# Block-causal attention and a three-way maximum feed-forward: the first product in chunks of 512 tokens, with the last 64 tokens of each batch kept for a ninth chunk

## The chip, the cores and the metric

The kernel runs on one NeuronCore of a Trainium2 chip. The metric is the device time of one execution in microseconds, the median of several runs. The engines go by their profile names: PE (TensorE matmul) and PEld (its weight loads), DVE (VectorE), ACT (ScalarE), POOL (GpSimd), SP (SyncE, which issues most DMAs).

## What is computed

```python
# q, k, v: (8 batches, 8 heads, 576 tokens, 64)
scores = 0.125 * q @ k.T            # per batch and head
scores = where(query_block >= key_block, scores, -1e9)   # blocks of 64 tokens
attn = softmax(scores) @ v
x = attn as (8 * 576 tokens, 512)   # heads side by side
h = maximum(maximum(x @ w1, x @ w2), x @ w3)             # w1..w3: (512, 768)
out = h @ w_out                                          # w_out: (768, 512)
```

A batch has 576 tokens, which is 512 + 64.

## The kernel before

**Attention.** Two heads form a `Pair` (four pairs a batch). For each pair the kernel loads q, k and v (`load`), turns q and k (`turn_qk`), and computes the scores of query tiles 3, 2, 0 and, later, 1 (`qk`, L933) and of the last 64 queries of both heads (`qk4`, L940). VectorE finds the row extremes with the mask (`top`, `top4`, L422), ScalarE takes exponentials (L606, L960), the sums are inverted (L746, L750), the rows scaled on ScalarE or GpSimd (L438, L440), and VectorE turns the result into a buffer `pz` (`turn`, L629, L633). Four DMAs on SP move each head's `pz` into `pt` with its partitions exchanged (`move`, L641). The value product (`pv`, L1000) gives the attention output transposed, features by tokens, in two halves: half 0 is 256 tokens, half 1 the other 320 (`HALF`). In the steady part one job, `both`, runs the value product of the previous pair and then the scores of tile 1 of the current one. There are two buffers of `pz` and two of `pt`; a pair uses both, one a head.

**Feed-forward.** All matrix products there are split in a high and a low part (`xh`, `xl`; `wh`, `wl`), three matmuls for one. `finish` copies the value product from PSUM to `x32`, casts it to `xh` on ScalarE and subtracts to get `xl` on GpSimd. A `Chunk` is one batch and one half: for each of 6 blocks `f` of 128 columns of the three weights and each weight `i`, four pairs `c` and three parts make 12 matmuls (`product`, L1118), 216 a chunk, over 256 or 320 tokens. `most` copies the first of three results to `m` (ScalarE) and takes the maximum with the other two (VectorE, L1133). `high` and `low` split `m` into `hh` and `hl`, with a reordering of its tokens in the access pattern; the last 64 tokens of a batch, which lie in half 1, go to a buffer `left` beside those of the next batch, so that two batches fill one tile of 128. `project` (L1184) multiplies tiles of 128 tokens by `w_out`, 18 matmuls of 512 columns a tile; `get` and `put` bring the result through `osb` to memory (L1209).

**Weights.** 18 `Unit`s for w1..w3 and 6 for w_out load a block as 64-bit words and make both parts from it: `size` (ScalarE), five VectorE steps `clamp` to `rest`, a cast, a product on TensorE (`whole`, L345 to L347) and a last copy. They use free `wo` buffers and `left` on the way; the last two w_out units (`dst` 4 and 5) use both `osb`.

**Order.** Nothing is ordered by hand. Each piece of work is a `Job` with estimated costs on the engines that can run it, a rank, its predecessors, and buffers that it takes and gives. `in_order` simulates the engines, starts on each idle engine the ready job of the lowest rank, and so fixes every engine's program. One rank unit is meant as about a microsecond. A pair starts at rank `rank`, 24 after the one before (`PAIR`); its predecessor's value product stands 9 later (`SECOND`). Batch 0 is made in two parts, `FRONT` (256 tokens, 8 apart) and `BACK` (20 apart), batch 1 is `EARLY`, the others are `WHOLE`. A chunk's products are spread evenly over ranks from the end of the batch's attention plus `END`, so chunk b-1 runs among the attention of batch b. The buffers `xh` and `xl` of one half hold one batch (four pairs): they are given back at the chunk's last product (`join`, L1083), one half after the other.

Of the kernel before, what the change touches and what calls it, by code (L numbers as in the profile page):

```python
# [18 lines left out]
NEG = -1.0e30  # L19
# [135 lines left out]
def kernel(  # L155
# [33 lines left out]
    XB = 2  # L189
    END = 24  # L190
# [3 lines left out]
        x32_0=XB, x32_1=XB, xh0=4, xl0=4, xh1=4, xl1=4, m=2, osb=2, left=1, qn=2, kn=2,  # L194
        vn=2, kq=2, q8=2, pz=2, pt=2,
# [8 lines left out]
    psa = ctx.enter_context(tc.tile_pool(name="psa", bufs=slots["sb"], space=PSUM))  # L204
    psm = ctx.enter_context(tc.tile_pool(name="psm", bufs=slots["pm"], space=PSUM))
# [3 lines left out]
    q8s = [const.tile([P, P], F32, name=f"q8_{n}") for n in range(2)]  # L209

    vns = [const.tile([P, 5 * P], F32, name=f"vn_{n}") for n in range(2)]
    for n in range(2):
        nc.gpsimd.memset(q8s[n], 0.0)
        nc.gpsimd.memset(vns[n][64:P, 4 * P :], 0.0)
# [3 lines left out]
    mask = const.tile([P, 1024], F32, name="mask")  # L218
    nc.gpsimd.memset(mask, 0.0)
    nc.gpsimd.memset(mask[0:64, 960:1024], NEG)  # L220
# [36 lines left out]
    class Unit:  # L257


        def __init__(self, u, src, dst, n, prior, *early, first=None):  # L260
# [6 lines left out]
            self.temps = (f"wo{u % NF}",) if not self.last else (f"wo{4 + dst % 2}",) if dst < 4 else ("osb", "osb")  # L267
# [19 lines left out]
            j = job({"PE": 6 * pe(512)}, rank, self.whole, after=(j,), take=("pm",), give=(*self.temps, "left"))  # L287
# [8 lines left out]
        def size(self, eng):  # L296
            if len(self.temps) == 1:
                w = moe.tile([P, 2, 512], F32, name=self.temps[0], bufs=1)
                self.a, self.b = w[:, 0], w[:, 1]
            else:  # L300
                self.a, self.b = (moe.tile([P, 512], F32, name="osb", bufs=slots["osb"]) for _ in range(2))
            nc.scalar.activation(self.a, self.high_word.bitcast(F32), AF.Abs)
# [32 lines left out]
        def rest(self, eng):  # L335
            parts = moe.tile([P, 2, NF, P], F32R, name="left", bufs=1)
            self.c = parts[:, 0, 0:4].rearrange("p f q -> p (f q)")
            nc.vector.scalar_tensor_tensor(  # L338
                out=self.c, in0=self.low_word, scalar=2.0**-52, in1=self.b, op0=ALU.mult, op1=ALU.mult
            )  # L340
# [57 lines left out]
    class Part:  # L398


        def __init__(self, first, later, halves, keys, queries, run, beside=False, plain=False):
# [6 lines left out]
            self.last, self.beside = queries.stop == S, beside  # L408
# [4 lines left out]
    WHOLE = Part(((3,), (2, 0)), (1,), (1, 0), S, slice(0, S), slice(0, RUN), True)  # L413
    EARLY = Part(((3,), (2, 0)), (1,), (1, 0), S, slice(0, S), slice(0, RUN))

    FRONT = Part(((1, 0),), (), (0,), 256, slice(0, 256), slice(0, 96), plain=True)
    BACK = Part(((3,), (2,)), (), (1,), S, slice(256, S), slice(96, RUN))
# [3 lines left out]
    def least(ps, hidden, first, out_):  # L421
        nc.vector.tensor_tensor_reduce(  # L422
# [19 lines left out]
    class Head:  # L442
# [63 lines left out]
        def plain_turns(self, t0):  # L506
# [31 lines left out]
            if part.last:  # L538
                if self.j == 0:
                    pair.raised = [  # L540
                        job({"PE": RAISE * n}, t0 + 12, pair.raise4, a, after=(pair.scaled, gate), take=("sb",))
                        for a, n in ((0, 4), (1, 1))
                    ]
                    join(pair.raised, ("p4",))
                for a, n in ((0, 256), (1, 64)):
                    place(self.place4, a, n=n, after=pair.raised[a])
                if self.j == 1:
                    for a in range(2):
                        join([h.placed[-2 + a] for h in heads], ("sb",))
# [11 lines left out]
        def turned_p(self):  # L561
            if not hasattr(self, "pt"):
# [5 lines left out]
                else:  # L568
                    z = att.tile([P, 4 * (RUN + 16)], F32, name="pz", bufs=slots["pz"])
# [10 lines left out]
        def place4(self, eng, a):  # L580
            step = PLACE[4][1]
            n = 1 if a else 4
            at = PLACE[4][0] + (288 if a else 0)
            src = self.pair.ps[a].rearrange("p (k i h c) -> p k i h c", i=4, h=2, c=16)[:, :, :, self.j]
            if a:
                dst, src = self.turned_p()[:, :, at : at + 16], src[:, 0]
            else:
                at += 16 - step
                dst = self.turned_p()[:, :, at : at + step * n].rearrange("p i (k u) -> p k i u", u=step)[:, :, :, step - 16 :]
            copy(eng, dst, src)  # L590

        def top(self, eng, t):
# [5 lines left out]
            least(self.ps[t], mask[:, 1024 - P * (t + 1) :], INF, self.stat[0][:, COL[t] : COL[t] + 1])  # L598
# [14 lines left out]
        def turn(self, eng, t):  # L613

            if not hasattr(self, "pz"):
                if self.j and self.pair.part.loads == 1:
                    self.pz = self.pair.heads[0].pz
                else:
                    self.pz = att.tile([P, 4 * (RUN + 16)], F32, name="pz", bufs=slots["pz"])
            z = self.pz.rearrange("p (j u) -> p j u", u=RUN + 16)  # L620
# [6 lines left out]
            a += self.off  # L627
            dst = z[:, :, a : a + step * n].rearrange("p j (k u) -> p k j u", u=step)[:, :, :, u : u + 32]
            nc.vector.transpose(dst, p[:, 0 : n * P])  # L629
            if t == 4:  # L630
                src = p[:, n * P : S].rearrange("p (j o r) -> p j o r", o=1, r=16).broadcast_to([P, 4, 2, 16])
                a += 288
                nc.vector.transpose(z[:, :, a : a + 32].rearrange("p j (o r) -> p j o r", r=16), src)  # L633

        def move(self, eng):
# [3 lines left out]
            z = self.pz.rearrange("p (j u) -> p j u", u=RUN + 16)  # L639
# [5 lines left out]
    class Pair:  # L645
# [3 lines left out]
        def __init__(self, b, hp, part, n):  # L649
            self.b, self.hp, self.part = b, hp, part  # L650
            self.heads = [Head(self, j) for j in range(2)]
            self.x32, self.o, self.xs, self.ps, self.began = [None, None], {}, {0: [], 1: []}, {}, None
# [3 lines left out]
            self.vn, self.q8 = vns[n % 2].rearrange("p (c h d) -> p c h d", h=2, d=D), q8s[n % 2]  # L656
# [128 lines left out]
        def plain_qk(self, rank, loads):  # L785

            part, o = self.part, self.at // P
            if part.loads == 1:
                banks = ((((o, o + 1, 4 + o, 5 + o), ((0, 0, 256),)),))
            else:  # L790
                a = part.queries.start // P
                own = tuple(range(a, 4))
                banks = [((4, 5, 6, 7), ((0, 2, 512),))]
                if a:
                    banks.append(((*own, 8), ((0, 1, P * len(own)), (P * len(own), 0, 64))))
                else:
                    banks += [(own, ((0, 1, 512),)), ((8,), ((0, 0, 64),))]
# [41 lines left out]
        def finish(self, prior, r, priors={}):  # L839
            self.xjobs = {}  # L840
            for half in self.part.halves:
                n = HALF[half]
                done = job(
                    {"ACT": act(n), "DVE": dve(n)},
# [4 lines left out]
                    take=(f"x32_{half}",),  # L849
                    give=("sb",),  # L850
                )
                h = job({"ACT": act(n, False)}, r + 4, self.x_high, half, after=(done,), take=(f"xh{half}",))
                self.xjobs[half] = job(
                    {"POOL": pool(n)}, r + 4, self.x_low, half, after=(h,), take=(f"xl{half}",), give=(f"x32_{half}",)
                )
            join((prior,), (self.tag,) * self.part.loads + ("vn",))
# [88 lines left out]
        def top4(self, eng, a):  # L945
# [5 lines left out]
            least(self.ps[a], mask[:, 0 : 64 if a else 512], nm[:, 0:1] if a else INF, nm[:, a : a + 1])  # L951

        def exp4(self, eng):
            nm, sm, _ = self.stat
            self.p4 = att.tile([P, 640], F32, name="p4", bufs=slots["p4"])
# [23 lines left out]
        def raise4(self, eng, a):  # L979

            z = self.ps[a] = psa.tile([P, P if a else 512], F32, name="sb")
            for c in range(1 if a else 4):
                src = self.p4[:, c * P : c * P + P]
                if a:
                    src = self.p4[:, 512:640]
                nc.tensor.transpose(z[:, c * P : c * P + P], src, plus.bitcast(F32))

        def scale4(self, eng):
            rs = self.stat[2][:, 0:1]
            normalise(eng, self.p4[:, 0:S], rs)  # L990
            if self.part.plain:
                nc.gpsimd.tensor_copy(self.p4[:, S:640], self.p4[:, 512:S])
# [15 lines left out]
        def out(self, eng, half):  # L1008
            self.x32[half] = att.tile([P, HALF[half]], F32, name=f"x32_{half}", bufs=slots[f"x32_{half}"])
            copy(eng, self.x32[half], self.o[half])  # L1010

        def x_high(self, eng, half):
            xh = xp.tile([P, HALF[half]], F32R, name=f"xh{half}", bufs=slots[f"xh{half}"])
            copy(eng, xh, self.x32[half])
            self.xs[half] = [xh]

        def x_low(self, eng, half):
            xl = xp.tile([P, HALF[half]], F32R, name=f"xl{half}", bufs=slots[f"xl{half}"])
            minus(eng, xl, self.x32[half], self.xs[half][0].bitcast(F32))
            self.xs[half].append(xl)  # L1020
# [4 lines left out]
    left = {}  # L1025

    class Chunk:


        def __init__(self, b, half, pairs, prior, start, end):  # L1030
            self.b, self.half, self.pairs, self.n = b, half, pairs, HALF[half]
# [246 lines left out]
```

## Time and profile before

| quantity | value |
|---|---|
| median of 3 runs | 929.71 us (929.12 to 930.51) |
| span of the profiled execution, first to last instruction | 929.0 us |
| mean granted TensorE clock of that execution | 0.989 |
| products in chunks (L1118) | 3456 matmuls |
| projection (L1184) | 648 matmuls |
| HBM read, written | 41.94 MB, 9.44 MB |

The time of the profiled execution itself is not recorded beside its span; the median of the other runs lies 0.7 us above the span. In the slices of the page each digit is the busy share of a fortieth of the span in tenths. In the groups of instructions the columns are line, engine, operation, output and input, shape and count, then the total busy time, the mean duration in ns, and the idle time before them with what ended it. Durations of neighbouring matmuls overlap, so the distance of their starts is the price of one, not the mean duration.

### The profile page before, as it was taken

The numbers are of one execution on the slowest core, as the hardware profiler recorded it, in microseconds if no ns is written. First come the engines' busy times: TensorE is split into PE (matmuls) and PEld (weight loads), VectorE is DVE, ScalarE is ACT, GpSimd is POOL, SyncE is SP. The second block draws the span as 40 slices with busy tenths as digits, with TensorE's granted clock in tenths as the row PEclk, the third lists the DMA queues.
The fourth block names the chain that finished last, engine by engine and source line by source line (L and its number), as shares of the span: only waits on it lengthen the run. The fifth ranks groups of instructions, "written<-read, shape, count | busy, mean of one in ns | idle before, by whom it ended". The sixth has DMA issues, their size and how long they took to land.

```text
span 929.0 us, 16751 instructions
## 1 busy us (share of the span) xinstructions
PE 892.9 (96%) x5776; PEld 737.4 (79%) x5776; DVE 537.7 (58%) x1568; ACT 472.2 (51%) x1339; POOL 247.0 (27%) x372
## 2 busy tenths in 40 slices
PE   6799798999999999999999999999999999999998
PEld 4466555777788888888888888888888888899997
DVE  4999987786674645565574655465564655431101
ACT  3876464666454555556364555556464655522111
POOL 3442222333231222214131222223131222222201
PEclk9999898999999999999999999999999999999999
DMA  7676654675554555555443554555543543330010
GB/s 199 161 232 144 137 165 99 154 147 127 117 120 107 111 120 109 132 110 122 107 86 86 113 124 102 131 111 132 109 95 76 113 117 84 95 72 23 2 35 24
DMA packets 238038, 103.36 MB, mean 111 GB/s; under 512 B 197504, under 2 KB 230272, under 8 KB 237952
## 3 DMA queue, kind: packets, MB, share of 16 engines
q1 hardware_dynamic: 217472, 87.33, 42.2%
q0 software_dynamic: 3456, 12.58, 4.0%
q10 hardware_dynamic: 17024, 2.36, 1.5%
q8 instruction: 46, 0.75, 0.3%
q14 instruction: 40, 0.33, 0.1%
HBM read 41.94 MB, written 9.44 MB: 55 GB/s over the span
## 4 chain that ended last, share of the span: by engine, by line
PE 84%; DVE 7%; DMA 4%; ACT 1%; issue 1%; SPq 1%; POOL 0%; ACTq 0%; DVEq 0%; POOLq 0%
PE pm L1118 46%; PE pm L1184 16%; PE sb L1000 10%; PE sb L933 8%; DMA pt<-pz 3%; PE sb L940 3%; DVE sb L422 1%; SPq L641 1%; ACT p L606 1%; DVE wo L321 1%; DVE wo L308 1%; PE pm L345 1%; DVE kq L917 1%; DVE left L338 1%; DVE pz L629 1%
## 5 line engine op out<-in xcount | busy, mean ns | idle before, releaser
L1118 PE MATMUL pm<-xh,w 128*128 128x320 f32 (+1 forms) x2304 | 499.8, 304 | 10.1 <-ACT w L249 6.9
L1118 PEld LDWEIGHTS pm<-xh,w 128*128 128x128 f32 x2304 | 379.4, 190 | 30.2 <-issue 14.9
L1118 PE MATMUL pm<-xl,w 128*128 128x256 f32 (+1 forms) x1152 | 341.6, 297 | 1.8 <-POOL xl L254 1.8
L1118 PEld LDWEIGHTS pm<-xl,w 128*128 128x128 f32 x1152 | 219.0, 190 | 9.2 <-issue 5.3
L422 DVE CUSTOM_DVE_ANT_0 sb<-sb,mask 128x512 f32<-128x512 f32 (+3 forms) x288 | 144.7, 529 | 131.9 <-PE sb L940 69.5
L1133 DVE TENSOR_TENSOR m<-pm,m 128x256 f32<-128x256 f32 (+1 forms) x192 | 87.2, 454 | 165.5 <-PE pm L1118 156.7
L606 ACT ACTIVATE p<-sb,nm 128x512 f32<-128x512 f32 (+3 forms) x256 | 134.1, 527 | 74.9 <-DVE nm L422 64.4
L629 DVE STREAM_TRANSPOSE pz<-p 128x512 f32<-128x512 f32 (+1 forms) x304 | 152.0, 535 | 22.2 <-ACT p L438 19.1
L254 POOL TENSOR_TENSOR hl<-m,hh 128x256 fp32r<-128x256 f32 x96 | 71.0, 739 | 326.4 <-ACT hh L249 294.7
L440 POOL TENSOR_TENSOR p<-p,rs 128x384 f32<-128x384 f32 (+4 forms) x128 | 91.9, 739 | 184.4 <-DVE rs L750 175.0
L1184 PE MATMUL pm<-wo,hh 128*128 128x512 f32 x384 | 119.6, 392 | 0.1
L1000 PE MATMUL sb<-pt,vn 128*64 128x320 f32 (+4 forms) x880 | 100.5, 370 | 5.8 <-DMA pt<-pz 4.9
L438 ACT ACTIVATE p<-p,rs 128x256 f32<-128x256 f32 (+4 forms) x160 | 88.8, 602 | 22.9 <-DVE rs L750 12.7
L249 ACT CAST hh<-m 128x256 fp32r<-128x256 f32 x96 | 39.0, 406 | 118.8 <-DVE m L1133 118.2
L1000 PEld LDWEIGHTS sb<-pt,vn 128*64 128x64 f32 x880 | 60.9, 140 | 44.1 <-issue 9.5
L933 PE MATMUL sb<-kq 64*128 64x384 f32 (+3 forms) x512 | 91.6, 477 | 2.6 <-DVE kq L251 2.0
L254 POOL TENSOR_TENSOR xl<-x,xh 128x256 fp32r<-128x256 f32 (+1 forms) x64 | 52.6, 828 | 148.8 <-ACT xh L249 148.8
L1184 PEld LDWEIGHTS pm<-wo,hh 128*128 128x128 f32 x384 | 70.9, 188 | 15.2 <-ACT wo L249 0.4
L933 PEld LDWEIGHTS sb<-kq 64*128 64x128 f32 x512 | 47.4, 197 | 39.5 <-issue 23.1
L1184 PE MATMUL pm<-wo,hl 128*128 128x512 f32 x192 | 74.9, 390 | 0.0
L249 ACT COPY m<-pm 128x256 f32<-128x256 f32 (+1 forms) x96 | 38.3, 399 | 43.4 <-PE pm L1118 31.8
L249 ACT COPY osb<-pm 128x512 f32<-128x512 f32 x36 | 21.1, 586 | 70.7 <-PE pm L1184 70.7
(79 smaller groups left out, 711.2 us busy)
## 6 DMA issues: line engine op xcount, KB each, us to landing
pt<-pz SPq DMA_DIRECT2D x224, 200.0 KB, 3.9
w<-in_moe_w_dram POOLq DMA_DIRECT2D x18, 512.0 KB, 5.1
nat<-in_k_dram SPq DMA_DIRECT2D x128, 72.0 KB, 2.5
vn<-in_v_dram SPq DMA_DIRECT2D x64, 128.0 KB, 2.4
out_dram<-osb SPq DMA_DIRECT2D x32, 256.0 KB, 2.0
nat<-in_q_dram SPq DMA_DIRECT2D x96, 72.0 KB, 2.9
pt<-pz SPq DMA_DIRECT2D x32, 152.0 KB, 3.9
wo<-in_moe_w_out_dram POOLq DMA_DIRECT2D x6, 512.0 KB, 4.8
```

Of the source, the lines that this page charges most:

```text
L249: nc.scalar.copy(dst, src)
L254: {"DVE": nc.vector, "POOL": nc.gpsimd}[eng].tensor_tensor(out=dst, in0=a, in1=b, op=ALU.subtract)
L422: nc.vector.tensor_tensor_reduce(out=ps, in0=ps, in1=hidden, scale=-SCALE, scalar=first, op0=ALU.add, op1=ALU.min, accum_out=out_)
L438: nc.scalar.mul(p, p, r)
L440: nc.gpsimd.tensor_tensor(out=p, in0=p, in1=r.broadcast_to([P, p.shape[1]]), op=ALU.mult)
L606: nc.scalar.activation(dst, src, AF.Exp, bias=nm[:, c : c + 1], scale=-1.0, accum_out=sm[:, c : c + 1])
L629: nc.vector.transpose(dst, p[:, 0 : n * P])
L933: nc.tensor.matmul(ps, self.q[h.own, P * t : P * (t + 1)], self.k[h.own, 0:w], start=True, stop=True)
L1000: nc.tensor.matmul(o[h.own].rearrange("p (i u) -> p i u", u=n)[:, :, c0 : c0 + z - a], self.vn[:, kt, h.j, :], h.pt[:, :, h.off + a : h.of ...
L1118: nc.tensor.matmul(self.ps, w[i, f][:, c, :], xx, start=(c == 0 and s == 0), stop=(c == NC - 1 and s == 2))
L1133: nc.vector.tensor_tensor(out=m, in0=ps, in1=m, op=ALU.max)
L1184: nc.tensor.matmul(self.po[: self.rows], h, w[f], start=(f == 0 and s == 0), stop=(f == NF - 1 and s == 2))
```

## The change

Chunks are no longer halves of a batch. Batch 0 has a chunk of tokens 0 to 255 and one of 256 to 511, batches 1 to 7 one of 512 each, and a ninth chunk at the end has the last 64 tokens of all eight batches. Their attention output is stored to memory by `save` as each pair ends, and `Rest` loads and splits it at the end.

```diff
-    XB = 2
-    END = 24
+    XB = 3
+    END = 34
-        x32_0=XB, x32_1=XB, xh0=4, xl0=4, xh1=4, xl1=4, m=2, osb=2, left=1, ... q8=2, pz=2, pt=2,
+        x32=2 * XB, x=NP, m=3, ... q8=1, pz=2, pt=2,
+    rests = [hbm.tile([P, 64 * B], F32, name=f"rest{c}") for c in range(NP)]
-    mask = const.tile([P, 1024], F32, name="mask")
+    mask = const.tile([P, 320], F32, name="mask")
...
-            self.temps = (f"wo{u % NF}",) if not self.last else (f"wo{4 + dst % 2}",) if dst < 4 else ("osb", "osb")
+            self.temps = (f"wo{u % NF}",) if not self.last else (f"wo{4 + dst % 2}",) if dst < 4 else ("pz",)
-                j = job({"DVE": c}, rank, step, after=(j,), take=("left",) if step == self.rest else (), lasts=c + GAP)
+                j = job({"DVE": c}, rank, step, after=(j,), take=("m",) if step == self.rest else (), lasts=c + GAP)
```

A value product is copied into one `x32` tile for both halves; a pair's `xh` and `xl` hold 512 tokens, in the order of the output, and the one set of them is given back at the last product of a chunk that ends at token 512.

```diff
+            done = [
+                job({"ACT": act(HALF[half]), "DVE": dve(HALF[half])}, r + 2, self.out, half,
+                    after=(priors.get(half, prior),), take=("x32",) * (2 // len(part.halves)), give=("sb",))
+                for half in part.halves
+            ]
+            if part.last:
+                rest = job({"SP": LOAD}, r + 6, self.save, after=(*done, saved.get(self.hp)), lasts=LOAD + DMA)
+                saved[self.hp] = rest
+            whole = part.rows.start == 0
+            h = job({"ACT": act(n, False)}, r + 4, self.x_high, after=done, take=("x",) if whole else ())
+            self.xjob = job({"POOL": pool(n)}, r + 4, self.x_low, after=(h,))
+            join((self.xjob, rest), ("x32", "x32"))
...
+        def save(self, eng):
+            nc.sync.dma_start(
+                rests[self.hp][:, 64 * self.b : 64 * self.b + 64].rearrange("p (i c) -> p i c", i=4), self.x32[:, :, 0:16]
+            )
...
+        def tokens(self, t):
+            t = t[:, self.part.rows]
+            return t.rearrange("p (s i c) -> p i s c", i=4, c=32)
...
+        def x_high(self, eng):
...
+            copy(eng, self.tokens(self.xs[0]), self.firsts())
```

`Rest` loads the 512 stored tokens of a pair into attention buffers (`pz`, `pt`, `p3`) after the last value product. `hh`, `hl` and `m` become 512 wide, the reordering in `high` and `low` goes, `left` and `osb` go, and the output of the projection passes through `m`.

```diff
-            join((last,), [f"x{s}{half}" for s in "hl"] * NC)
+            if rows.stop == 512:
+                join((last,), ("x",) * NC)
...
-                        after=(prior, *self.done[NF - 1 if f == 0 else f], units["out", f].done),
+                        after=(prior, self.done[max(f, NF - 2)], units["out", f].done),
...
-                a = job({"ACT": act(DO)}, NOW, self.get, tt, after=(prior,), take=("osb",), give=("pm",))
+                a = job({"ACT": act(DO)}, NOW, self.get, tt, after=(prior,), take=("m",), give=("pm",))
...
-            middle = start + (rank + END - start) * HALF[1] / S
-            chunks += [(b - 1, 1, pairs[b - 1], start, middle), (b - 1, 0, pairs[b - 1], middle, rank + END)]
+            chunks.append((slice(0, 512), tiles(b - 1, 3, 2, 0, 1), before, start, rank + END))
...
+    chunks.append((slice(0, 512), tiles(B - 1, 3, 2, 0, 1), before, start, end))
+    ends = [rest := Rest(c, rank + SECOND + 2 * PAIR + c, rest) for c in range(NP)]
+    own = [tuple((b * S + 512, 64 * (b % 2), 64) for b in (2 * tt, 2 * tt + 1)) for tt in range(B // 2)]
+    chunks.append((slice(0, 512), own, ends, end, end + PAIR * NP * 2 / 3))
```

The rest of the diff makes room: the mask is 320 columns and read with overlapping or repeated steps, `pz` loses its padding, `q8` has one buffer instead of two, and code of `plain` parts that no part used is taken out. The score, exponential, turn and value-product instructions stay, on the same shapes.

More of the change, by code (lines that the diff above doesn't have):

```diff
@@ L188 @@
     NEAR = 4
-    XB = 2
-    END = 24
+    XB = 3
+    END = 34
     slots = dict(
         sb=5, sb5=4, scores=4, pm=3, stat=2, stat4=2, p0=2, p1=2, p2=2, p3=2, p4=1,
-        x32_0=XB, x32_1=XB, xh0=4, xl0=4, xh1=4, xl1=4, m=2, osb=2, left=1, qn=2, kn=2,
-        vn=2, kq=2, q8=2, pz=2, pt=2,
+        x32=2 * XB, x=NP, m=3, qn=2, kn=2, vn=2, kq=2, q8=1, pz=2, pt=2,
     )
@@ L398, with __init__ @@
     class Part:
-        def __init__(self, first, later, halves, keys, queries, run, beside=False, plain=False):
+        def __init__(self, first, later, halves, keys, queries, run, rows, beside=False, plain=False):
             self.first, self.later = first, later
@@ L537, in plain_turns @@
                 join((place(self.place, t, n=P * (t + 1), after=up),), ("sb",))
[L538 to L549, printed above, removed]
             self.moved = join(self.placed, ())
@@ L597, in top @@
             self.stat = tuple(t[:, self.j] for t in pair.stats)
[L598 removed]
+            least(self.ps[t], hidden(t), INF, self.stat[0][:, COL[t] : COL[t] + 1])
         def exp(self, eng, t):
@@ L787, in plain_qk @@
             part, o = self.part, self.at // P
[L788 to L797, printed above, removed]
+            banks = ((((o, o + 1, 4 + o, 5 + o), ((0, 0, 256),)),))
             ups, downs = [], []
@@ L839, in finish @@
         def finish(self, prior, r, priors={}):
[L840 to L844, printed above, removed]
+            part, self.ended = self.part, prior
+            n, rest = part.rows.stop - part.rows.start, None
+            done = [
+                job(
+                    {"ACT": act(HALF[half]), "DVE": dve(HALF[half])},
                     r + 2,
@@ L848, in finish @@
                     after=(priors.get(half, prior),),
-                    take=(f"x32_{half}",),
+                    take=("x32",) * (2 // len(part.halves)),
                     give=("sb",),
                 )
[L852 to L856, printed above, removed]
+                for half in part.halves
[7 more added lines that the diff above has]
+            join((self.xjob, rest), ("x32", "x32"))
+            join((prior,), (self.tag,) * part.loads + ("vn",))
         def values(self, eng):
@@ L1008, in out @@
         def out(self, eng, half):
[L1009 to L1020, printed above, removed]
+            part = self.part
@@ new lines, in out @@
+            if self.x32 is None:
+                w = sum(HALF[h] for h in part.halves) // 4
+                self.x32 = att.tile([P, S], F32, name="x32", bufs=XB)[:, 0 : 4 * w].rearrange("p (i u) -> p i u", i=4)
+            n = HALF[half] // 4
+            a = HALF[1] // 4 if half == 0 and part.last else 0
+            copy(eng, self.x32[:, :, a : a + n], self.o[half].rearrange("p (i u) -> p i u", i=4))
+        def save(self, eng):
+            nc.sync.dma_start(
+                rests[self.hp][:, 64 * self.b : 64 * self.b + 64].rearrange("p (i c) -> p i c", i=4), self.x32[:, :, 0:16]
+            )
@@ new lines, in tokens, with firsts @@
+        def tokens(self, t):
+            t = t[:, self.part.rows]
+            return t.rearrange("p (s i c) -> p i s c", i=4, c=32)
+        def firsts(self):
+            a = 16 if self.part.last else 0
+            return self.x32[:, :, a:].rearrange("p i (s c) -> p i s c", c=32)
+        def x_high(self, eng):
+            if self.part.rows.start == 0:
+                self.xs = [xp.tile([P, 512], F32R, name=nm, bufs=NP) for nm in ("xh", "xl")]
+            else:
+                self.xs = made[self.hp].xs
+            copy(eng, self.tokens(self.xs[0]), self.firsts())
@@ new lines, in x_low, with __init__, room, part @@
+        def x_low(self, eng):
+            xh, xl = (self.tokens(t) for t in (self.xs[0].bitcast(F32), self.xs[1]))
+            minus(eng, xl, self.firsts(), xh)
+    class Rest:
+        def __init__(self, c, first, prior):
+            self.c, self.prior = c, prior
+            fresh = c in (0, 3)
+            j = job(
+                {"SP": LOAD},
+                first,
+                self.load,
+                after=(saved[c], made[-1].ended, prior and prior.loaded),
+                take=("pz",) if fresh else (),
+                lasts=LOAD + DMA,
+            )
+            self.loaded = j
+            j = self.highs = job(
+                {"ACT": act(512, False)},
+                first,
+                self.high,
+                after=(j, prior and prior.highs),
+                take=(("pt",) if c == 0 else ("p3",)) if fresh else (),
+            )
+            self.xjob = job(
+                {"POOL": pool(512)},
+                first,
+                self.low,
+                after=(j, prior and prior.xjob),
+                take=(("pt",) if c == 0 else ("p3",)) if fresh else (),
+            )
+        def room(self, nm, dtype):
+            if self.c == 0 or (self.c == 3 and nm == "pz"):
+                return att.tile([P, 4 * RUN], dtype, name=nm, bufs=2)
+            return att.tile([P, 512], dtype, name="p3", bufs=slots["p3"])
+        def part(self, t):
+            return t[:, 512 * (self.c % 3) :][:, 0:512]
+        def load(self, eng):
+            self.z = self.room("pz", F32) if self.c in (0, 3) else self.prior.z
+            nc.sync.dma_start(self.part(self.z), rests[self.c])
+        def high(self, eng):
+            t = self.h = self.room("pt", F32R) if self.c in (0, 3) else self.prior.h
+            self.xs = [self.part(t)]
+            copy(eng, self.xs[0], self.part(self.z))
+        def low(self, eng):
+            t = self.l = self.room("pt", F32R) if self.c in (0, 3) else self.prior.l
+            self.xs.append(self.part(t))
+            minus(eng, self.xs[1], self.part(self.z), self.xs[0].bitcast(F32))
@@ L1024, with __init__ @@
     NOW = -1.0e3
-    left = {}
     class Chunk:
-        def __init__(self, b, half, pairs, prior, start, end):
-            self.b, self.half, self.pairs, self.n = b, half, pairs, HALF[half]
+        def __init__(self, rows, tiles, pairs, prior, start, end):
+            self.rows, self.tiles, self.pairs, self.n = rows, tiles, pairs, rows.stop - rows.start
             self.hs = {}
             cols = self.n
-            step = (end - start) / (3 * NF * NC + 12 * cols / DO * 3 * NF * NC / 36)
-            after = {}
-            xjobs = [p.xjobs[half] for p in pairs]
-            spare, spared = cols > 256, None
+            one = pe(*[cols] * 3)
+            step = (end - start) / (3 * NF * NC + len(tiles) * NF * pe(*[DO] * 3) / one)
+            xjobs = [p.xjob for p in pairs]
@@ L1066, in __init__ @@
                     )
[L1067 to L1081 removed]
+                h = job({"ACT": act(cols, False)}, NOW, self.high, f, after=(ev,), take=(f"hh{f}",))
+                self.done[f] = job({"POOL": pool(cols)}, NOW, self.low, f, after=(h,), give=("m",))
             self.last = last
[L1083 removed]
+            if rows.stop == 512:
+                join((last,), ("x",) * NC)
             rank = start + step * 3 * NF * NC
             prior = None
[L1087 to L1093 removed]
+            for tt in range(len(tiles)):
                 for f in range(NF):
@@ L1109, in __init__ @@
                 join((prior,), (f"hh{f}",))
-            if tiles[-1] >= 2:
-                join((prior,), ("left",))
         def product(self, eng, f, i, c):
@@ L1115, in product @@
                 self.ps = psm.tile([P, self.n], F32, name="pm")
-            xh, xl = self.pairs[c].xs[self.half]
+            xh, xl = (t[:, self.rows] for t in self.pairs[c].xs)
             for s, (w, xx) in enumerate(((wh, xh), (wh, xl), (wl, xh))):
@@ L1221, in plan, with tiles @@
         return pairs
+    def tiles(b, *ts):
+        return [((b * S + P * t, 0, P),) for t in ts]
     rank = 0
```

193 lines of the change are left out of this document (59 added, 134 removed).

## The prediction

> **What bounds the kernel now.** I read the page from the top: the busy times, the forty slices, the chain that ended last.
>
> ```profile
> span 929.0 us, 16751 instructions
> PE 892.9 (96%) x5776; PEld 737.4 (79%) x5776; DVE 537.7 (58%) x1568; ACT 472.2 (51%) x1339; POOL 247.0 (27%) x372
> PE   6799798999999999999999999999999999999998
> PEclk9999898999999999999999999999999999999999
> PE 84%; DVE 7%; DMA 4%; ACT 1%; issue 1%; SPq 1%; POOL 0%; ACTq 0%; DVEq 0%; POOLq 0%
> ```
>
> TensorE is busy 96% of the span and holds 84% of the chain; no other engine is above 58%. Its idle time lies in the first slices. The view by stages sizes it (columns: length, PE busy, PEld, DVE, ACT, POOL, granted clock, DMA share, GB/s):
>
> ```profile
> 0.00:50.00 50.00, 34.77 (x150) 20.52 (x150) 35.64 (x107) 30.46 (x88) 20.99 (x35) 1.00 0.67 173
> 50.00:100.00 50.00, 46.25 (x267) 33.68 (x268) 48.96 (x110) 31.50 (x74) 19.86 (x24) 1.00 0.70 192
> 100.00:150.00 50.00, 39.40 (x178) 24.89 (x176) 40.80 (x108) 28.72 (x72) 13.40 (x18) 0.84 0.54 134
> 150.00:200.00 50.00, 49.62 (x303) 39.23 (x301) 38.66 (x121) 29.03 (x92) 11.72 (x20) 0.99 0.67 146
> 200.00:300.00 100.00, 97.67 (x612) 78.41 (x611) 60.63 (x187) 54.77 (x163) 28.12 (x42) 0.98 0.55 120
> 300.00:400.00 100.00, 100.00 (x686) 84.69 (x686) 58.11 (x176) 53.96 (x157) 26.39 (x41) 1.00 0.51 110
> ```
>
> PE misses 29.6 us up to 150 us (15.2, 3.8, 10.6), 2.7 us in the next 150, and then nothing. So there are two regimes: a start-up of some 220 us in which weights and the first attention pairs set the time, and a long stretch in which each microsecond of matrix work is a microsecond of the kernel. A busy PE need not be at its peak, so the price of a matmul is read as the distance from one start to the next in the timeline's undisturbed end (columns: start, length, instruction):
>
> ```profile
> 850.84 0.46 PE L1118 MATMUL pm<-xh,w 128*128 128x320 f32 x2
> 851.13 0.31 PE L1118 MATMUL pm<-xl,w 128*128 128x320 f32 x1
> 851.28 0.46 PE L1118 MATMUL pm<-xh,w 128*128 128x320 f32 x2
> ```
>
> ```profile
> 907.04 0.40 PE L1118 MATMUL pm<-xh,w 128*128 128x256 f32 x2
> 907.28 0.28 PE L1118 MATMUL pm<-xl,w 128*128 128x256 f32 x1
> 907.40 0.40 PE L1118 MATMUL pm<-xh,w 128*128 128x256 f32 x2
> ```
>
> Three 256-wide products take 0.36 us (0.120 each), three 320-wide ones 0.44 (0.1467 each). No product is 512 wide yet; the nearest row is the projection, which has the same type, one weight load per matmul and 512 moving columns. The chain of waits gives it over long runs:
>
> ```profile
> 881.75 12.27 PE pm L1184 x54
> ...
> 917.05 8.20 PE pm L1184 x36
> ```
>
> 12.27/54 is 0.2272 and 8.20/36 is 0.2278; I take 0.2275. From 256 to 512 columns that is 0.42 ns a column, which leaves about 12.5 ns per matmul that do not depend on its width.
>
> **The change, part by part. Products.** Before, each of 8 batches takes 216 products of 320 and 216 of 256 columns: 216 x (0.1467 + 0.120) = 57.6 us, 460.9 us in all. After, batch 0 has two chunks of 256 (2 x 216 x 0.120 = 51.8) and eight chunks have 512 (8 x 216 x 0.2275 = 393.1): 445.0 us. The columns are the same; 1296 matmuls and their fixed part are gone. **-15.9 us** of PE work. The projection keeps its 36 tiles of 18 matmuls, attention keeps its matmuls.
>
> That is a gain only where PE is the bound, and 5.8 us of it (216 x 0.0267) lie in the second chunk of batch 0, in the start-up. There the attention of batch 1 is what is late. In the chain between 125 and 260 us its value products (L1000) stand at
>
> ```profile
> 167.70 2.86 PE sb L1000 x28
> ...
> 181.88 3.69 DMA pt<-pz
> ...
> 185.71 2.89 PE sb L1000 x22
> ...
> 202.06 2.86 PE sb L1000 x28
> ...
> 221.74 2.86 PE sb L1000 x28
> ...
> 242.09 4.57 PE sb L1000 x22
> ```
>
> From pair 0 (ends at 170.56) to pair 2 (204.92) a pair takes 17.2 us, and pair 1 stands behind the DMA that moves its turned probabilities, so this pace is the attention's own. Pair 3 could then start at 219.3; it starts at 221.7, after the projection. So the chunk's work covers the attention with only 2.4 us to spare. Shortened by 5.8 us it leaves PE idle for 5.8 - 2.4 = 3.4 us, since the next chunk needs all four pairs. **+3.4 us**; the ends are 0 (attention moves up by all of it) and 5.8.
>
> **Buffers in the start-up.** The last two weight units of `w_out` borrow a `pz` buffer instead of both `osb`, and the heads need the two `pz` for their turns. How long one is held:
>
> ```profile
> 139.60 0.69 ACT L302 ACTIVATE osb<-wo 128x512 f32<-128x512 f32 x1
> 149.61 0.67 ACT L302 ACTIVATE osb<-wo 128x512 f32<-128x512 f32 x1 [2.40 <-issue]
> 156.15 0.70 DVE L629 STREAM_TRANSPOSE pz<-p 128x512 f32<-128x512 f32 x1
> 159.20 0.40 PE L347 MATMUL pm<-left,plus 128*128 128x512 f32 x1
> ```
>
> The second unit runs from 149.6 to 159.6 and ranks ahead of the turn at 156.15 (second head of batch 1's first pair), which may wait up to 6 us: until the unit is through or the first head's move has landed. Against that, the units stop sharing the one `left` buffer and may overlap. Against it as well, the smaller mask shortens the first instructions:
>
> ```profile
> 1.77 0.95 POOL L219 MEMSET mask<- 128x1024 f32 x1
> ```
>
> at 320 columns about 0.3, so up to 0.65 us, which counts only if the weights behind it, on a VectorE that is 98% busy from 50 to 100 us, follow. `END` puts a chunk's products 10 rank units later against the attention, which changes their order and not their sum; it falls under the same ends. Ends: -3 (a tenth of the 29.6 us of early idling) and +6; as only one head of one pair is held and its value product had slack, I take **+2 us**.
>
> **Casts and evictions.** The strided reordering moves from `hh` to `xh`, and all evictions become 512 wide:
>
> ```profile
> L254 POOL TENSOR_TENSOR xl<-x,xh 128x320 fp32r<-128x320 f32 x32 | 28.4, 889 | 116.0 <-ACT xh L249 116.0
> L254 POOL TENSOR_TENSOR xl<-x,xh 128x256 fp32r<-128x256 f32 x32 | 24.3, 767 | 32.8 <-ACT xh L249 32.8
> L249 ACT CAST w<-wo 128x512 fp32r<-128x512 f32 x18 | 11.1, 617 | 7.1 <-DVE left L338 5.3 <-DVE pz L629 1.6
> ```
>
> POOL goes from 767 to 889 ns for 64 more columns, so a 512-wide `xl` is about 1.25 us; the ACT cast is 0.62. They lie beside PE. Their cover matters at one place: the `x` buffers of a batch now come free in one piece, at the last product of the chunk before, so all casts of the next batch fall between two chunks. Four times 1.25 us on POOL, behind the first 0.62, is under 6 us, and a fourth pair waits in PSUM until an `x32` buffer is free; the projection of the old chunk (72 x 0.2275 = 16.4 us) runs meanwhile. I cost it at **0**. Without that cover a turn would cost PE the 3.5 us from a value product through two copies, a cast and one `xl`. At the end of the kernel the same holds: maximum, cast and `hl` of the last block take about 3 us after the last product, and the projection reaches that block after 5 x 3 x 0.2275 = 3.4.
>
> **The saved tokens** add 32 stores and 4 loads on SP. SP already stands waiting:
>
> ```profile
> SPq L902 <- PE sb L1000: 197.3, 30, 12.0
> ```
>
> A store waits for the copies just behind the value product, and the next loads and the pz-to-pt moves stand behind it; they share that wait already, so what is new is one issue, 0.6 us, per pair. Ends 0 and 0.6 on the pair's loop; hidden, **0** (the loop is a rival below). The ninth chunk reads its data over 100 us after the last store. Its output tiles are two half tiles, so the kernel ends with two DMAs:
>
> ```profile
> L1209 SPq DMA_DIRECT2D out_dram<-osb x2: 368/460/552, 162.3 to 166.4; - x2
> ...
> out_dram<-osb SPq DMA_DIRECT2D x32, 256.0 KB, 2.0
> ...
> out_dram<-osb SPq DMA_DIRECT2D x8, 128.0 KB, 2.3
> ```
>
> One more issue (0.5) and 2.3 for 2.0 us to land: **+0.8 us**.
>
> **Sum:** -15.9 + 3.4 + 2.0 + 0.8 = -9.7 us. The profiled execution spans 929.0 us and lies 0.7 below the median of 929.7; I keep that distance: **920.0 us**. With the two start-up terms at their lower ends (0 and -3) it is 911.6, at their upper ends (5.8 and 6) 926.4.
>
> A rule of the Trainium skill ("TensorE: Matmul & The Clock Gate", section "Back-to-back issue gap") speaks against the main term: an isolated warm matmul is followed by the next after N/2.4 plus about 2.5 ns. By it 1296 matmuls would save an estimated 3.2 us instead of 15.9, and the sum would be 932.7. The three widths of this trace show a fixed part of 12 to 14 ns, so here I go by the rows.
>
> **The rivals.**
>
> *All of it arrives.* Batch 1's attention moves up and the units lose nothing: 929.7 - 15.9 + 0.8 = 914.6. For it: PE had almost no gap from 160 to 220 us. Against: the DMA at 181.88, behind which a value product stood. 0.17.
>
> *A longer start-up.* Both terms at their upper ends, plus 1.3 us because both halves of a pair must be cast before a product: 929.7 - 15.9 + 5.8 + 6 + 1.3 + 0.8 = 927.7. 0.08.
>
> *The pair loop becomes the bound* (slower). One pair's later scores wait for its predecessor's value product, and its own value product for its moved transposes. Where nothing covered it, that loop took 242.09 - 221.74 = 20.35 us. In the steady stretch a batch takes 103.4 us, read from the fourth pair's value product of batch 2 to that of batch 6:
>
> ```profile
> 317.78 2.86 PE sb L1000 x28
> ...
> 731.60 2.86 PE sb L1000 x28
> ```
>
> That is 413.8 us for four batches. Minus 10.5 us of PE work a batch (57.6 + 18.4 before against 49.1 + 16.4 after), 103.4 falls to 92.9, or 23.2 us a pair. The loop then has 2.9 us to spare where it had 5.5. If stores on SP, longer casts and blocked PSUM push it past that, 28 pairs pay the excess: from 23.6 us on the gain is gone (28 x 0.4 = 11.2), at 24.0 the time is 920 + 22 = 942. A wait also costs more than itself:
>
> ```profile
> 240.00:260.00 20.00, 17.98 (x112) 14.68 (x112) 11.62 (x33) 7.94 (x25) 3.00 (x6) 0.91 0.52 104
> ```
>
> the gap of 2.0 us at 240 stands in a window with the clock at 0.91, and the value product behind it took 4.57 for 2.86 us. Against it: pairs at 23 us (294.74 to 317.78) ran without a gap of PE. 0.13.
>
> *The fixed part grows with the width*: products cost by the column and 512 wide ones hold no saving: 929.7 + 6.2 = 935.9. The projection's rows speak against it. 0.04; it is the case towards which the skill's smaller figure points.
>
> **How the numbers follow.** A measurement of this kernel tells some 0.2% (1.9 us) from no change. Forecast 0.58, full gain 0.17, long start-up 0.08 (half of it within 0.2%), loop 0.13 (0.02 within 0.2%), width 0.04. Faster 0.58 + 0.17 + 0.04 = 0.79, same 0.06, slower 0.15. The range goes from 911.5, the low end of the sum, to 929.5, which takes in the long start-up and a loop that stalls now and then; the loop in full and the width, 0.17, stay outside.
>
> **What would show it.** Products: 2160 of them, 512-wide starts 0.2275 us apart; at 0.24 the main term is gone. Start-up: 3 to 6 us more PE idle between 140 and 230 us, before the first 512-wide product, and the two `w_out` units beside a late turn. Steady stretch: PE busy 100% and value products of a batch's last pairs 93 us apart; gaps released by the pz-to-pt DMA would show the loop, gaps released by `xl` the turn of the buffers. End: two stores behind the last copy. The forecast is wrong if the steady stretch shows PE gaps, or if the start-up shifts by more than 6 us either way.

## The result and the profile after

| | before | after |
|---|---|---|
| median, same session | 930.11 us (929.12 to 933.14) | 906.19 us (905.23 to 907.34) |
| ratio to before, 95% interval | | 0.9749 (0.9725 to 0.9772) |
| span of the profiled execution | 929.0 us | 905.0 us (its own time 906.73) |

The change is worth 23.9 us, where 9.7 were forecast, and the time lies below the stated range. One execution of the kernel with split products below took 4465.28 us where the others took some 927; the ratio leaves it out. First the page of the changed kernel: busy times, slices and chain.

```profile
span 905.0 us, 13891 instructions
PE 873.5 (97%) x4480; PEld 647.0 (71%) x4480; DVE 531.6 (59%) x1502; ACT 439.1 (49%) x1205; POOL 232.5 (26%) x247
PE   6889988999999999999999999999999999999997
PEclk9999999999999999999999999999999999999999
PE 85%; DVE 7%; DMA 4%; issue 1%; SPq 1%; ACT 1%; POOL 0%; ACTq 0%; DVEq 0%; POOLq 0%
```

Of the 24.0 us between the spans, PE's busy time gives 19.4 (892.9 to 873.5) and its idle time 4.6 (36.1 to 31.5). The products explain some 14 to 16 us of the busy time (below). The rest of the gain lies in the start-up, where the forecast had put costs. The clock row (`PEclk`), which had an 8 in the fifth slice, has none now. By stages (columns as in the prediction):

```profile
100.00:150.00 50.00, 41.74 (x211) 28.43 (x212) 46.68 (x126) 30.56 (x79) 13.41 (x17) 0.97 0.61 148
150.00:200.00 50.00, 49.27 (x347) 38.79 (x347) 45.16 (x135) 32.52 (x102) 13.95 (x19) 1.00 0.78 165
200.00:300.00 100.00, 100.00 (x529) 72.34 (x528) 69.45 (x208) 57.73 (x167) 33.04 (x32) 1.00 0.64 134
300.00:400.00 100.00, 100.00 (x511) 73.92 (x510) 58.83 (x177) 53.47 (x152) 25.34 (x25) 1.00 0.58 128
```

From 100 to 150 us VectorE is busy 46.7 us where it was 40.8, and the granted clock is 0.97 for 0.84. The value products (L975 now), the matmuls that turn a pair's probabilities into its attention output, show in the chain of waits what came of it:

```profile
155.37 2.86 PE sb L975 x28
...
172.89 2.96 PE sb L975 x26
...
189.71 2.89 PE sb L975 x22
...
204.08 2.86 PE sb L975 x28
...
225.36 3.56 PE sb L975 x24
```

The first pair of batch 1 comes at 155.4 us; before it was 167.7. Pair 0 of batch 2 comes at 225.4, before 242.1. From there on the steady stretch does what was forecast: PE is full, and behind 170 us the view of waits lists one wait of PE, of 0.7 us. The same pair of successive batches, further down in the chain of the changed kernel:

```profile
355.86 2.86 PE sb L975 x28
...
449.15 2.86 PE sb L975 x28
```

A batch takes 93.29 us (forecast 92.9, before 103.4).

### The profile page after: what moved, and what is told of

Same layout as the page of the kernel before. It is cut to its first block, busy times and chain, and to the rows that moved or that the text cites. A ratio compares the mean times of both kernels' runs of the same rounds, so it can differ in the third digit from the quotient of the medians.

```text
span 905.0 us, 13891 instructions
## 1 busy us (share of the span) xinstructions
PE 873.5 (97%) x4480; PEld 647.0 (71%) x4480; DVE 531.6 (59%) x1502; ACT 439.1 (49%) x1205; POOL 232.5 (26%) x247
## 4 chain that ended last, share of the span: by engine, by line
PE 85%; DVE 7%; DMA 4%; issue 1%; SPq 1%; ACT 1%; POOL 0%; ACTq 0%; DVEq 0%; POOLq 0%
PE pm L1141 48%; PE pm L1170 16%; PE sb L975 9%; PE sb L919 8%; DMA pt<-pz 3%; PE sb L926 3%; DVE sb L434 1%; DVE pz L617 1%; DVE m L349 1%; DVE wo L333 1%; DMA nat<-in_q_dram 1%; DVE wo L320 1%; SPq L631 1%; DVE wo L339 1%; DMA vn<-in_v_dram 0%
## 5 line engine op out<-in xcount | busy, mean ns | idle before, releaser
L1141 PE MATMUL pm<-xh,w 128*128 128x512 f32 (+1 forms) x1296 | 401.4, 381 | 2.5 <-ACT w L260 1.9
L1141 PEld LDWEIGHTS pm<-xh,w 128*128 128x128 f32 x1296 | 237.3, 189 | 59.6 <-issue 14.7
L1141 PE MATMUL pm<-xl,w 128*128 128x512 f32 (+1 forms) x648 | 238.0, 367 | 0.0
L434 DVE CUSTOM_DVE_ANT_1 sb<-sb,mask 128x512 f32<-128x512 f32 (+2 forms) x224 | 127.6, 590 | 96.7 <-PE sb L926 59.5
L452 POOL TENSOR_TENSOR p<-p,rs 128x256 f32<-128x256 f32 (+4 forms) x112 | 95.5, 870 | 342.8 <-DVE rs L740 165.9
L1155 DVE TENSOR_TENSOR m<-pm,m 128x512 f32<-128x512 f32 (+1 forms) x120 | 76.1, 634 | 170.2 <-PE pm L1141 169.3
L617 DVE STREAM_TRANSPOSE pz<-p 128x384 f32<-128x384 f32 (+1 forms) x304 | 151.7, 536 | 36.8 <-POOL p L452 16.9
L594 ACT ACTIVATE p<-sb,nm 128x128 f32<-128x128 f32 (+3 forms) x256 | 133.1, 529 | 73.1 <-DVE nm L434 58.8
L1141 PEld LDWEIGHTS pm<-xl,w 128*128 128x128 f32 x648 | 123.0, 190 | 22.5 <-issue 5.0
L450 ACT ACTIVATE p<-p,rs 128x384 f32<-128x384 f32 (+4 forms) x176 | 88.2, 555 | 36.1 <-DVE rs L740 31.8
L975 PE MATMUL sb<-pt,vn 128*64 128x320 f32 (+4 forms) x880 | 97.2, 361 | 6.4 <-DMA pt<-pz 5.1
L975 PEld LDWEIGHTS sb<-pt,vn 128*64 128x64 f32 x880 | 59.5, 137 | 47.0 <-issue 11.5
```

Of the source, the lines that this page charges most:

```text
L434: nc.vector.tensor_tensor_reduce(out=ps, in0=ps, in1=hidden, scale=-SCALE, scalar=first, op0=ALU.add, op1=ALU.min, accum_out=out_)
L450: nc.scalar.mul(p, p, r)
L452: nc.gpsimd.tensor_tensor(out=p, in0=p, in1=r.broadcast_to([P, p.shape[1]]), op=ALU.mult)
L594: nc.scalar.activation(dst, src, AF.Exp, bias=nm[:, c : c + 1], scale=-1.0, accum_out=sm[:, c : c + 1])
L975: nc.tensor.matmul(o[h.own].rearrange("p (i u) -> p i u", u=n)[:, :, c0 : c0 + z - a], self.vn[:, kt, h.j, :], h.pt[:, :, h.off + a : h.of ...
L1141: nc.tensor.matmul(self.ps, w[i, f][:, c, :], xx, start=(c == 0 and s == 0), stop=(c == NC - 1 and s == 2))
```

## The experiments

Three theories were set up for the start-up. A: `END` at 34 changed the order of products and scores. B: the weight units no longer stand in line for the one `left` buffer. C: the shorter second chunk itself. The first experiment is apart from them and asks what a matmul, with its weight load, costs besides its columns.

### One product as two of half the width

```diff
-                nc.tensor.matmul(self.ps, w[i, f][:, c, :], xx, start=(c == 0 and s == 0), stop=(c == NC - 1 and s == 2))
+                for a in range(0, self.n, 256):
+                    nc.tensor.matmul(
+                        self.ps[:, a : a + 256], w[i, f][:, c, :], xx[:, a : a + 256],
+                        start=(c == 0 and s == 0 and a == 0), stop=(c == NC - 1 and s == 2 and a + 256 == self.n),
+                    )
```

> Every 512-wide product matmul becomes two of 256 columns into the two halves of the same PSUM tile; the order of work, the buffers and the number of chunks stay. Theory 1 (a fixed part of 12.5 ns per matmul, read from the starts 0.120 us apart at 256 columns and 0.2275 at 512): 8 x 216 = 1728 more matmuls cost 21.6 us, 906.2 becomes 928, with no new idling of PE. Rival (the fixed part grows with the width, the gain of the change came from elsewhere): 906 to 908.

Measured: 926.97 us, ratio to before 0.9948 (0.9931 to 0.9965). The medians lie 20.8 us above the change's, the spans (922.8 and 905.0) 17.8. In the chain of waits of this kernel a batch takes

```profile
315.95 2.86 PE sb L975 x28
...
411.53 2.86 PE sb L975 x28
```

95.58 us, 2.29 more than in the changed kernel, for 216 more matmuls: 10.6 ns each. Over 1728 matmuls the medians give 12.0 and the spans 10.3. PE has no more idle time: 100.00 of 100 us in each window from 300 us on. So the fixed part exists at 10.6 to 12.0 ns, and the 1296 matmuls that the change drops were worth 13.7 to 15.6 us. The rival (906 to 908) falls.

At the end of the kernel PE runs products alone, and the chain gives their price directly: the chunk of batch 7 first, then the ninth chunk. In the changed kernel

```profile
769.82 48.28 PE pm L1141 x213
...
834.42 49.46 PE pm L1141 x216
```

and with split products

```profile
783.37 51.11 PE pm L1142 x426
...
850.83 50.88 PE pm L1142 x432
```

In the chunk of batch 7 a 512-wide product takes 0.2267 us (0.2275 was forecast) and two halves 0.2400, so one matmul more costs 13.3 ns; in the ninth chunk these are 0.2290 and 0.2356, 6.6 ns. Why the ninth differs is open. The smaller figure of the Trainium skill ("TensorE: Matmul & The Clock Gate", "Back-to-back issue gap"), which the page gives for an isolated matmul, does not hold for this kernel's stream.

### The changed kernel with END at 24

```diff
-    END = 34
+    END = 24
```

> The changed kernel with END back at 24; everything else stays. Theory A (order: in the start-up the products of the second chunk stand ahead of the scores of batch 1's second pair on PE, wait there for a cast, and hold the turn of the first pair on DVE; END 34 put them behind): about 10 to 12 us of the start-up gain are lost, 916 to 918, and the first WHOLE value product (pair 0 of batch 2, after at 225 us) comes at about 236. Theory B (the weight units no longer share the one left buffer): 906. Theory C (the shorter second chunk itself, 256 for 320 columns): 906.

Measured: 919.54 us, ratio 0.9883 (0.9859 to 0.9908). The size is that of theory A, but not the place. The chain of waits of this kernel:

```profile
155.72 2.86 PE sb L975 x28
...
231.56 2.89 PE sb L975 x22
...
422.77 2.89 PE sb L975 x22
...
517.84 2.89 PE sb L975 x22
```

Batch 1's first pair comes at 155.7 as in the changed kernel. Pair 0 of batch 2 does come 6.2 us later (231.6 for 225.4), about half of what theory A named, but most of that is order and not lost time: from 100 to 250 us PE is idle for 10.4 us where it was 9.0. The larger loss is in the steady stretch, where a batch takes 95.07 us (422.77 to 517.84) instead of 93.29, 1.8 us more in each of six batches: some 11 of the 13.2 us between the spans. At the pair where one chunk ends and the next begins, the chain shows a DMA before the value product:

```profile
418.22 4.42 DMA pt<-pz
422.63 0.14 issue
422.77 2.89 PE sb L975 x22
```

PE's waits from 250 to 800 us (columns: total us, times, longest) are, in the main,

```profile
PE sb L975 <- DMA pt<-pz: 1.9, 3, 1.0
PE sb L919 <- ACT p L594: 1.8, 5, 0.4
```

The value product before starts at 402.76, 20.0 us earlier, and in between the chain goes through VectorE's turns, the moves on SP and their DMA. This is the prediction's pair loop, where 20.35 us was read, at the one pair of a batch that spans the turn. The next ones, at 442.73, 462.65 and 498.14, come without a wait of PE. PE has products to run for nearly all of the 20 us; it waits for 0.9. All its waits from 250 to 800 us come to 4.8 us, 0.8 to 0.9 a batch, which is half of the 1.8. The other half lies in time that the profile counts as busy, and its cause is open. At `END` 34 PE has no such waits. So theory A falls for the start-up.

### The changed kernel with the units in line again

```diff
-... take=("m",) if step == self.rest else () ...
+... take=("m", "one") if step == self.rest else () ...
...
-... give=(*self.temps, "m"))
+... give=(*self.temps, "m", "one"))
...
-        x32=2 * XB, x=NP, m=3, ...
+        x32=2 * XB, x=NP, m=3, one=1, ...
```

> The changed kernel with one more token, of which there is one, taken by a weight unit together with its m buffer and given back with it, so that units stand in line as they did for the one left buffer; nothing else changes. Theory B: the start-up loses some 8 to 10 us, 914 to 916. Theory A: within 3 us of 906. Theory C: 906.

Measured: 915.27 us, ratio 0.9827 (0.9800 to 0.9853): 9.1 us by the medians and 7.3 by the ratios (0.0078 of 930) are lost. The chain of waits:

```profile
164.43 3.10 PE sb L975 x24
...
237.29 2.89 PE sb L975 x22
```

Now the start-up is what is late: 164.4 and 237.3 where the changed kernel had 155.4 and 225.4. Up to 250 us PE is idle for 32.0 us where it was 26.8, and the granted clock up to 100 us is 0.93 for 1.00. Theory B holds, A and C miss.

### The kernel before with END at 34

```diff
-    END = 24
+    END = 34
```

> The kernel before with END at 34 and nothing else changed. Theory A: the start-up gain appears without the change, 930 becomes 918 to 920. Theories B and C: within 3 us of 930.

Measured: 930.37 us, ratio 1.0003 (0.9989 to 1.0017). Its first value product of batch 1 stands at 168.21 us. `END` does nothing for the kernel before that the interval shows; theory A misses here too.

### The kernel before with two buffers for the units, and with one

```diff
-                j = job({"DVE": c}, rank, step, after=(j,), take=("left",) if step == self.rest else (), lasts=c + GAP)
+                j = job({"DVE": c}, rank, step, after=(j,), take=("uc",) if step == self.rest else (), lasts=c + GAP)
...
-            parts = moe.tile([P, 2, NF, P], F32R, name="left", bufs=1)
-            self.c = parts[:, 0, 0:4].rearrange("p f q -> p (f q)")
+            self.c = moe.tile([P, 512], F32R, name="uc", bufs=slots["uc"])   # uc=2, or uc=1
...
```

In both kernels the unit's product on TensorE gives this buffer back, and both have the small mask of the change, to make room.

> The kernel before, with two buffers of their own for the value that a weight unit keeps from its last VectorE step to its product on TensorE, in place of the one left buffer (the small mask of the change goes with it to make room). Theory B (units in line behind one buffer set the start-up): 930 becomes 919 to 922, and the value product of batch 1's first pair moves from 167.7 us to 155 to 160. Rival D (the start-up differs by an accident of the planned order, and the one buffer is not its cause): within 4 us of 930, either way.

> The same with one such buffer, apart from left: the line of the units is as long as before, only left and the mask are changed. Theory B: within 3 us of 930. Rival D: anything from 920 to 935.

Measured with two: 918.70 us against 931.34 in the same session, ratio 0.9870 (0.9846 to 0.9895). With one: 931.06 us, ratio 0.9997 (0.9981 to 1.0014). The second buffer alone is worth 12.6 us of the kernel before, a little over what theory B said (919 to 922), and neither the small mask nor the separation from `left` is worth anything that the interval shows. The value products move as theory B said, in the kernel with two buffers to

```profile
155.66 2.86 PE sb L1008 x28
...
230.90 2.89 PE sb L1008 x22
```

With one buffer the first stands at 167.09. Rival D (an accident of the order) is left without support: the line costs time in both kernels, and taking it away gains in both. The stretch from 100 to 160 us, of the kernel before, then of the one with two buffers, then of the change:

```profile
100.00:160.00 60.00, 49.40 (x227) 32.83 (x225) 48.74 (x127) 31.25 (x77) 13.40 (x18) 0.86 0.53 127
```

```profile
100.00:160.00 60.00, 54.43 (x282) 37.49 (x282) 52.22 (x140) 37.44 (x98) 18.45 (x25) 0.97 0.63 154
```

```profile
100.00:160.00 60.00, 51.74 (x285) 35.86 (x287) 56.26 (x151) 37.92 (x102) 16.33 (x21) 0.97 0.63 148
```

VectorE (third number) is idle for 11.3 us of the 60 before, for 7.8 with two buffers, for 3.7 after, and PE does 282 and 285 matmuls where it did 227. PE's clock goes from 0.86 to 0.97. The kernel with two buffers spans 915.6 us, 13.4 less than before:

```profile
PE 888.5 (97%) x5776; PEld 734.8 (80%) x5776; DVE 536.9 (59%) x1570; ACT 472.0 (52%) x1337; POOL 247.6 (27%) x372
```

With the same 5776 matmuls PE is busy for 4.4 us less and idle for 9.0 less.

Who waits for whom in the start-up of the kernel before was there to be read in the view of waits up to 168 us (columns: total us, times, longest):

```profile
ACT wo L249 <- PE pm L347: 7.7, 4, 2.7
PE pm L1118 <- ACT w L249: 6.9, 4, 4.9
...
DVE left L338 <- PE pm L347: 5.9, 3, 3.5
...
ACT w L249 <- DVE left L338: 5.3, 6, 2.2
```

`left` is written by VectorE's last step (L338) and free again after TensorE's last product of the unit (L347). So the next unit's step waits for PE (5.9 us), ScalarE's cast for that step (5.3), and the products of the first chunk for the weights (6.9). In the changed kernel the last two of these read

```profile
ACT w L260 <- DVE m L349: 5.8, 8, 1.2
...
PE pm L1141 <- ACT w L260: 1.9, 3, 0.9
```

VectorE's step does not wait for PE at all there, nor in the kernel with two buffers, and the products wait for the weights 1.9 us (1.4 with two buffers). ScalarE's wait for the step is as long as before, so it does not come from the one buffer. With one buffer of its own (`uc`=1) the three read 5.3, 5.3 and 6.9, much as before. Neither of the two waits that shrink, by 5.9 and 5.0 us, reaches the 12.6 us. `in_order` fixes each engine's program, so the attention that stands behind a wait there is held up with it; that this makes up the rest is argued, not shown.

### END at 44

> The changed kernel with END at 44. With END 24 each turn from chunk to chunk left PE a gap of about 0.9 us and a batch took 95.3 us for 93.3. Theory (at a turn the products of the next chunk need casts that can begin only at the last product of the chunk before, and the last pair's value product must be there by then; END sets which of both is early): at 44 the products end later, the last pair's output waits in PSUM instead, PE has products to run, 905 to 908. Rival (blocked PSUM holds up the attention): a gap per turn again, 912 or more.

Measured: 907.59 us, ratio 0.9753 (0.9734 to 0.9772), the same as at 34 within the intervals, as the theory said; the rival's 912 or more misses. The time is flat between 34 and 44.

### The stores twice

```diff
+            for to in (rests, again):
+                nc.sync.dma_start(to[self.hp][:, 64 * self.b : 64 * self.b + 64] ..., self.x32[:, :, 0:16])
```

> The changed kernel with each of the 32 stores of the last 64 tokens issued twice, the second to a tensor that nobody reads. If the stores are hidden (my forecast put them at 0): 906 to 907. Rival (an issue of 0.6 us lies on the pair's loop for 28 pairs): about 17 us more, 923.

Measured: 908.30 us, ratio 0.9756 (0.9736 to 0.9776), no difference that the intervals show. The stores and their issues are hidden.

### Two x32 tiles, and four m buffers

```diff
-    XB = 3
+    XB = 2
...
-... m=3, ...      # second kernel only
+... m=4, ...
```

> The changed kernel with x32 tiles for two pairs in place of three. The output of a batch's third and fourth pair then has to wait in PSUM until the last product of the chunk before has freed the x buffers. Theory (this one-piece turnover is what the third tile covers): the third pair's copy is held for up to a pair's time, two of five score banks with it, and each turn costs PE 1 us or more, 913 to 925. Rival (the projection of 16.4 us covers it anyway): 906 to 908.

> As e9, and the room goes into a fourth m buffer, which weight units, maxima and outputs share. Theory B (the units' line was the start-up's limit, and with three buffers VectorE is already 94% busy from 100 to 160 us): the start-up gains 2 us at most over e9. Rival (the line is still the limit): 5 us or more.

Measured: 908.44 us, ratio 0.9765 (0.9731 to 0.9800), and 908.07, ratio 0.9758 (0.9723 to 0.9792). My theory for the first, 913 or more, was wrong: two tiles do as well as three within the intervals, which fits the rival, that the projection covers the turn of the buffers. A fourth `m` buffer gives nothing more that the intervals show, as theory B expected: with three, the line no longer limits. No version tried beats the change.

## Why the prediction was wrong

**The bound** was read rightly: PE without a gap in the long stretch, 100.00 us of each 100 from 200 us on, a start-up with other limits.

**Products**, -15.9 us: the step holds. 13.7 to 15.6 measured, and a batch of 93.29 us for 92.9. The price of 0.2275 us for a product 512 wide, taken from the projection, was right within 1%.

**"Buffers in the start-up", +2 us with ends of -3 and +6: this is the step that failed, in sign and in size.** Two opposite edits were weighed in it, the borrowed `pz` and the end of the shared `left`, and the second was given "a tenth of the 29.6 us of early idling" as its most. It was the largest part of the start-up: -12.6 us in the kernel before, and 7 to 9 us lost in the changed one when it is taken back. The error was to take the start-up for work-bound, on the strength of a VectorE that is 98% busy from 50 to 100 us, when in the next 60 us VectorE was idle for 11. The waits that named the buffer, VectorE for PE (5.9 us) above all, were not read for who stood in line. The borrowed `pz`, the part that was priced, did no visible harm: the first pair of batch 1 is 12 us earlier in spite of it. It was not tried by itself.

**The second chunk too short to cover the attention**, +3.4 us: not confirmed, and one of its premises was wrong. The attention's own pace of 17.2 us a pair was no floor, since pair 3 now follows pair 2 by 14.4 us (189.71 to 204.08), and PE idles only 0.7 us between 150 and 300 us. Against the kernel with two unit buffers and a 320-wide second chunk, the changed kernel has 2.7 us more PE idle from 100 to 160 us (8.26 for 5.57), which would be this cost at another place. Up to 250 us 1.6 of them are left. That is argued from two spans, not shown. It fits that the two parts measured by themselves, 12.6 and 13.7 to 15.6, come to more than the 23.9 of the whole.

**The slow clock** was named only as a price of new gaps. It was also a part of what there was to gain: PE's busy time fell by 3.8 to 5.7 us more than the products explain, while the clock between 100 and 160 us rose from 0.86 to 0.97; with two unit buffers, where the matmuls stay as they were, it fell by 4.4.

**Casts and evictions at 0, stores at 0**: hold, by a PE that is full from 200 us on, by the kernels with two `x32` tiles and with doubled stores. **The end**, +0.8: the last copy starts at 900.33 us and the span ends at 905.0, 4.7 us later; before these were 925.27 and 929.0, 3.7. So about +1.0.

**The rivals.** "All of it arrives" at 914.6 was on the right side and still too high, since it took the start-up for fixed. The pair loop is real: at `END` 24 it shows at one pair of each batch, not at 28 pairs, and the kernel is 12 to 13 us slower. The forecast had `END` as an edit of order without a price, which was right only for the kernel before.

## What to carry to other kernels

In a start-up where several engines pass work in a ring, look for the buffer of which there is one: an engine that is nearly full in one window can stand idle in the next because the ring stops there. Price an edit that frees such a buffer from the waits that name it and from the work queued behind them, not as a share of the visible idling. In a stretch where PE is full, the width of a matmul is worth its fixed part times the matmuls saved, and this can be forecast within a few us from the distances of starts.

## What the runs showed of the hardware

A matmul of this kernel, with its weight load, costs 10.6 to 12.0 ns beside its columns, as split products showed in a stretch bound by PE, about what starts at two widths had given (12.5). Where products run alone it was 13.3 ns in one chunk and 6.6 in another. Stores to memory in runs of 64 bytes, 32 KB each, land in 2.0 us; the output's stores of 128 and 256 KB land in 2.3 and 2.5 in the same view, the DMA view of the kernel with doubled stores:

```profile
rest<-x SPq DMA_DIRECT2D x32, 32.0 KB, 2.0
again<-x SPq DMA_DIRECT2D x32, 32.0 KB, 1.9
```

PE's gaps can cost twice. From 100 to 160 us of the kernel before, PE was idle for 10.6 us, 4.9 of it in one wait, and ran at a mean granted clock of 0.86. The sum of the gaps does not set the clock by itself: in the same stretch it was 0.97 with 5.6 us idle (two unit buffers), 0.97 with 8.3 (the change) and 1.00 with 8.8 (the change with `END` 24), where no wait was longer than 2.0 us. The prediction's row from 240 to 260 us has 0.91 behind one gap of 2.0. No rule comes out of these rows.
